# Attention and a squared-ReLU feed-forward: from one interleaved pass with one level of Strassen's form to three stages with two levels

## The chip, the core and the metric

The kernel runs on one core of one Trainium2 chip. The metric is the device time of one execution in microseconds (us). The engines are PE (matrix products), DVE, ACT and POOL (element work), and SP (which issues the transfers). PE writes only to PSUM, which has eight banks of 128 x 512 numbers; DVE and ACT read PSUM, POOL works from SBUF. All numbers are 32-bit floats.

## The reference

```python
scores = (1 / 8) * q @ k.T                          # 8 batches, 8 heads, 576 tokens, head size 64
thresh = max(scores, axis=-1) - tau
attn = softmax(where(scores >= thresh, scores, -1e9))
x = (attn @ v), heads side by side                  # 4608 tokens x 512
h = maximum(x @ w_in, 0)                            # w_in 512 x 2048
out = (h * h) @ w_out                               # w_out 2048 x 512
```

q, k and v arrive as 32-bit numbers, the two weights as 64-bit numbers, which the kernel converts itself.

## The kernel before, in words

**Attention** goes by pairs of heads (32 pairs) and blocks of query tokens: four blocks of 128 and one of 64 per pair, so 160 slots. In a slot, `scores` puts the score blocks of both heads into PSUM. `softmax` takes the row maximum (DVE, L342), the exponential (ACT, L356), the threshold with the row sum (DVE, L362) and the division (POOL, L378). `transposes` turns the weights (PE, L395 and L406) and copies them to SBUF (ACT, L397 and L407). `values` multiplies with v (PE, L432 and L437), for two blocks (256 tokens) or the last three (320 tokens) at a time, and ACT copies the result into x (L445). `turn` turns q and k of the next pair (L285, L294).

**The feed-forward** goes by pieces of 256 tokens, 18 in all. Each layer uses one level of Strassen's form: seven block products in place of eight. In `feed_forward`, the first layer (L491) has 14 products of 8 matmuls with 128 columns, the second (L600) seven of 8 matmuls with 256 columns. Sums of operands (`combine_x`, the sums of g) and of results run on DVE and POOL (helpers at L185 and L188), the square on POOL (L502) or DVE (L500). Nothing of this goes through DRAM.

**The order.** In the first 34 slots (`early_slot`) the order on PE, DVE, ACT and POOL is written out by hand: in nearly every slot one chunk of the weights is loaded and converted in six steps (`convert1` to `convert6`), and sums of weight blocks follow. The score tiles take two times three banks, all other PSUM tiles share two. After that only PE's order is written by hand; the scores take four banks and the others four. There `run` places feed-forward products between the slots, as many as keep a steady share, so that PE has products to do while DVE, ACT and POOL work on attention. A 32-bit matmul shows in the trace as two instructions, each with its weight load (PEld).

## Time and profile before

| what | value |
|---|---|
| median of 3 runs | 1578.9 us (1576.45 to 1580.72) |
| the profiled execution, its own time | 1579.66 us |
| its span | 1577.9 us |
| mean granted PE clock | 0.987 of full |
| 0 to 200 us: busy PE, DVE, ACT, POOL | 169.2, 155.7, 144.0, 158.0 us |
| 200 to 1480 us: the same | 1250.8, 647.1, 443.1, 428.3 us |
| clock in these two stretches | 0.95, 0.99 |

The profile's lines are read like this. In a timeline: start and duration in us, engine, line, operation, output tile <- inputs, shapes, number of instructions, and in brackets how long the engine stood idle before and what released it. In a list of groups: number of instructions, then total busy time and mean ns of one, then the idle time before them. Busy times of PE overlap, since an instruction's modelled end lies after the start of the next; the pace of PE is read from start to start.

### The profile page before, as it was taken

To read this page: it belongs to the slowest core of one execution; us is meant where nothing else is said; L and a number is where in the kernel's file an instruction comes from. 1 tells how busy PE (TensorE), PEld (TensorE's weight loads), DVE (VectorE), ACT (ScalarE), POOL (GpSimd) and SP (SyncE) were. 2 spreads that over 40 slices of the span, in tenths; PEclk is the share of its full clock that TensorE was granted. 3 is DMA by queue.
4 is the path that set the end of the run, shared out by engine and by line. 5 is a ranking of instruction groups with operands and counts; after the bars stand their busy time and mean duration, and the time that the engine had idled before them with its cause. 6 is when DMAs were issued, how large, how long until landed. Compare 5 with 4: busy or idle time off the path is not lost.

```text
span 1577.9 us, 25866 instructions
## 1 busy us (share of the span) xinstructions
PE 1511.6 (96%) x10042; PEld 1203.8 (76%) x10042; DVE 829.1 (53%) x1748; ACT 597.1 (38%) x1285; POOL 611.3 (39%) x690
## 2 busy tenths in 40 slices
PE   6888989999999999999999999999999999999998
PEld 3455557878786878787878786878788787878988
DVE  6878884636454455554554544454645464533222
ACT  6867743334242433333334333333334333421100
POOL 4899782423232242423242423241424242333221
PEclk9999989999999999999999999999999999999999
DMA  5544301010100100010001010001010001000000
GB/s 154 150 126 133 111 23 37 16 37 9 37 24 22 30 22 24 23 30 23 22 23 37 24 29 23 22 23 37 17 36 23 25 21 30 8 14 1 15 14 14
DMA packets 107914, 58.70 MB, mean 37 GB/s; under 512 B 89872, under 2 KB 99088, under 8 KB 107792
## 3 DMA queue, kind: packets, MB, share of 16 engines
q1 hardware_dynamic: 107792, 57.04, 13.0%
q8 instruction: 80, 1.31, 0.3%
q14 instruction: 42, 0.34, 0.1%
HBM read 47.58 MB, written 9.44 MB: 36 GB/s over the span
## 4 chain that ended last, share of the span: by engine, by line
PE 79%; DVE 7%; POOL 7%; ACT 4%; issue 2%; DMA 0%; SPq 0%; ACTq 0%; DVEq 0%; POOLq 0%
PE ph L491 28%; PE po L600 26%; PE sc L326 10%; PE pwT L406 6%; PE pv L437 4%; POOL w L378 3%; DVE nmx L342 3%; ACT w L356 2%; PE pwR L395 2%; PE pv L432 1%; PE pqk L285 1%; DVE g L185 1%; DVE s L188 1%; DVE w L362 1%; ACT x L445 1%
## 5 line engine op out<-in xcount | busy, mean ns | idle before, releaser
L378 POOL TENSOR_SCALAR w<-w,sm 128x576 f32<-128x576 f32 (+1 forms) x320 | 236.0, 748 | 575.8 <-DVE sm L369 561.9
L342 DVE TENSOR_REDUCE nmx<-sc 128x1 f32<-128x576 f32 x288 | 206.4, 749 | 190.1 <-PE sc L326 180.6
L362 DVE SCALAR_TENSOR_TENSOR w<-sc,thr,w 128x576 f32<-128x576 f32 x288 | 225.0, 814 | 138.8 <-ACT w L356 125.6
L356 ACT ACTIVATE w<-sc,nmx 128x576 f32<-128x576 f32 x288 | 199.8, 741 | 241.4 <-DVE nmx L342 234.7
L600 PE MATMUL po<-w_out,g 128*128 128x256 f32 x1152 | 267.7, 386 | 11.9 <-DVE g L185 9.6
L600 PEld LDWEIGHTS po<-w_out,g 128*128 128x128 f32 x1152 | 217.9, 193 | 43.6 <-issue 9.8
L491 PE MATMUL ph<-x,w_in 128*128 128x128 f32 x1728 | 208.8, 277 | 0.5
L326 PE MATMUL sc<-kT,qT 64*128 64x512 f32 (+3 forms) x1164 | 203.6, 464 | 2.6 <-DVE w L362 2.2
L491 PEld LDWEIGHTS ph<-x,w_in 128*128 128x128 f32 x1728 | 202.2, 193 | 3.2 <-ACT wR L401 1.3
L326 PEld LDWEIGHTS sc<-kT,qT 64*128 64x128 f32 (+1 forms) x1164 | 93.3, 176 | 105.4 <-issue 89.0
L406 PE MATMUL pwT<-ident,w 128*128 128x128 f32 x1024 | 145.6, 279 | 11.6 <-ACT x L445 9.4
L407 ACT COPY wT<-pwT 128x512 f32<-128x512 f32 x256 | 144.6, 591 | 29.1 <-PE pwT L406 26.3
L491 PE MATMUL ph<-xt,s_in 128*128 128x128 f32 x1152 | 142.9, 278 | 0.2
L437 PE MATMUL pv<-wT,va 128*64 128x320 f32 (+1 forms) x1024 | 141.3, 419 | 0.0
L491 PEld LDWEIGHTS ph<-xt,s_in 128*128 128x128 f32 x1152 | 136.3, 194 | 1.3 <-ACT wT L407 1.2
L406 PEld LDWEIGHTS pwT<-ident,w 128*128 128x128 f32 x1024 | 114.9, 142 | 27.1 <-ACT x L445 17.5
L188 DVE TENSOR_TENSOR u<-ph,u 128x512 f32<-128x512 f32 x110 | 75.7, 690 | 111.2 <-PE ph L491 105.4
L600 PE MATMUL po<-t_out,g 128*128 128x256 f32 x576 | 131.9, 379 | 0.0
L437 PEld LDWEIGHTS pv<-wT,va 128*64 128x64 f32 x1024 | 69.5, 139 | 65.1 <-issue 27.9
L600 PEld LDWEIGHTS po<-t_out,g 128*128 128x128 f32 x576 | 107.9, 190 | 13.8
L502 POOL TENSOR_TENSOR g<-p 128x512 f32<-128x512 f32 x36 | 38.1, 1059 | 155.1 <-ACT p L555 155.1
L188 DVE TENSOR_TENSOR o<-po,u 128x256 f32<-128x256 f32 x54 | 22.9, 424 | 96.2 <-PE po L600 96.2
(86 smaller groups left out, 1667.6 us busy)
## 6 DMA issues: line engine op xcount, KB each, us to landing
kn<-in_k_dram SPq DMA_DIRECT2D x72, 128.0 KB, 2.9
va<-in_v_dram SPq DMA_DIRECT2D x36, 256.0 KB, 2.7
out_dram<-o SPq DMA_DIRECT2D x36, 256.0 KB, 2.0
raw<-in_moe_w_in_dram SPq DMA_DIRECT2D x16, 512.0 KB, 4.1
raw<-in_moe_w_out_dram SPq DMA_DIRECT2D x16, 512.0 KB, 3.6
qn<-in_q_dram SPq DMA_DIRECT2D x56, 128.0 KB, 2.4
rn<-in_q_dram SPq DMA_DIRECT2D x36, 32.0 KB, 2.4
rn<-in_k_dram SPq DMA_DIRECT2D x36, 32.0 KB, 2.6
```

Source lines behind the costliest of these rows:

```text
L188: e.tensor_tensor(out=out, in0=x, in1=y, op=ALU.add)
L326: nc.tensor.matmul(to, qT[rows, ds(t * P, m)], kT[rows, ds(k0, n)], start=True, stop=True)
L342: nc.vector.tensor_reduce(out=nmx[:, j : j + 1], in_=sc[:, ds(at[j], S)], axis=AXIS.X, op=ALU.max, negate=True)
L356: nc.scalar.activation(out=w[:, ts(j, S)], in_=sc[:, ds(at[j], S)], func=AF.Exp, bias=nmx[:, j : j + 1], scale=1.0)
L362: nc.vector.scalar_tensor_tensor(out=w[:, ts(j, S)], in0=sc[:, ds(at[j], S)], scalar=thr[:, j : j + 1], in1=w[:, ts(j, S)], op0=ALU.is_ge, ...
L378: nc.gpsimd.tensor_scalar(out=out, in0=w, scalar1=r, scalar2=1.0, op0=ALU.mult, op1=ALU.mult)
L406: nc.tensor.transpose(pt[:, c, :], w[:, ds(j * (S + REST) + c * P, P)], ident[:, :])
L407: nc.scalar.copy(wT[:, j, :, at], pt[:, :, :])
L437: nc.tensor.matmul(pv[rows, :], va[:, j, c, :], wT[:, j, c, 0:n], start=False, stop=(c == FULL - 1), skip_group_check=True,)
L491: nc.tensor.matmul(to[:, j, :], a, b, start=(not more and j == 0 and c == 0), stop=(c == 1), skip_group_check=True,)
L502: e.tensor_tensor(out=to, in0=c[:, :, :], in1=c[:, :, :], op=ALU.mult)
L600: nc.tensor.matmul(to[:, :], a[:, f, :], b[:, f, :], start=(not more and f == 0), stop=(f == KF - 1), skip_group_check=True,)
```

## The change

The work is put into three stages, one after the other, and the order on all engines is written by hand.

1. All 160 slots of attention, with no feed-forward between them. The three-bank score tiles and two shared banks stay to the end. `values` now runs in every slot, for one block, and its result goes to DRAM (`xT`). A slot's steps are spread over four slots (`slot`). Weight conversions come every 2.5 slots, first w_out, later w_in. The sums of weight blocks for two levels (`sums`, 44 per weight) run on POOL, one per slot. The 49 sums of w_out are written to DRAM (`keep`), because both sets use the same SBUF tiles.
2. The first layer for all tokens, in nine steps of 512. Each step has seven outer products (`OUTER`) of seven inner ones (`inner`), 49 in all, each of four matmuls with 128 columns. Results of inner products are added on DVE, those of outer products on POOL (`final`, `add`). The sums of x for the next step run on POOL (`prepare_x`). ACT does ReLU and square, and the result is written to DRAM (`gT`). In the last step ACT's queue loads the w_out tiles back.
3. The second layer, again nine steps of 49 products of four matmuls with 128 columns. The squares are loaded (`load_g`), and 44 sums of them per step, outer and inner, go to POOL and, every third, to DVE (`adder`). The sums that the next step needs are issued in the last three outer products of a step.

The diff, cut (removed functions are those of the kernel before that the text above names: `feed_forward`, `combine_x`, `run`, `early_slot`):

```diff
+    OUTER, INNER = (1, 2, 6, 7, 4, 5, 3), (1, 6, 2, 7, 5, 4, 3)
+    SUMS_A = ((plus, 5, 7, 4), (minus, 6, 5, 1), (minus, 3, 2, 6), (minus, 7, 1, 7))
+    SUMS_B = ((minus, 5, 7, 1), (minus, 6, 3, 5), (minus, 4, 2, 6), (minus, 7, 3, 7))
+    AT_A, AT_B = ((1, 2), (7, 4)), ((1, 7), (2, 3))
...
+    def sums(W, which, at, done):
+        first = [at[a][b] for a in range(2) for b in range(2)]
+        for op, o, x, y in which:
+            for k_ in first:
+                to = W[o, k_] if o == y else weight_tile(W, o, k_)
+                yield op(nc.gpsimd, to[:, :], W[x, k_][:, :], W[y, k_][:, :])
+        for m in OUTER:
+            for op, o, x, y in which:
+                to = W[m, o] if o == y else weight_tile(W, m, o)
+                yield op(nc.gpsimd, to[:, :], W[m, x][:, :], W[m, y][:, :])
+            done(m)
...
+    def keep(m):
+        for k_ in INNER:
+            w_dram[m, k_] = dram.tile([P, BANK], FP32, name=f"w{m}{k_}")
+            later.append((w_dram[m, k_][:, :], W_OUT[m, k_][:, :]))
...
+    def values(i, t):
...
+        q0, n = t * P, BLK[t]
...
+        nc.tensor.matmul(pv[:, :], vd[:, :], wR[:, 0:n], start=False, stop=True, skip_group_check=True)
+        x = sb.tile([P, P], FP32, tag="x", bufs=3, name="x")
+        nc.scalar.copy(x[:, 0:n], pv[:, :])
+        later.append((xT[b][ts(hp, P), ds(q0, n)], x[:, 0:n]))
...
+    def slot(n):
...
+        values_and_load(n - 2)
+        turn_part(n - 1, "R")
+        stage(n + 2)
+        turn_part(n - 1, "W")
+        turn_part(n - 1, "w")
+        turn_begin(n)
+        stage(n + 1)
+        second(n + 1)
+        second(n + 2)
+        ahead(n + 3)
+        stage(n + 2)
+        second(n + 2)
+        turn_on(n, 0)
+        turn_on(n, 1)
+        stage(n + 1)
+        convert4(begun(3))
+        convert5(begun(3))
+        convert1(begun(1))
+        convert2(begun(1))
+        sums_step()
+        convert3(begun(2))
+        convert6(begun(4))
...
+    def inner(product, copy, temp, bank, final, tick):
...
+        X = bank()
+        product(X, 1, False)
+        p1 = temp("p1")
+        copy(p1, X)
+        tick(0)
+        Y = bank()
+        product(Y, 6, False)
+        u2 = temp("u2")
+        plus(nc.vector, u2, Y, p1)
+        tick(1)
+        product(X, 2, True)
+        final((0, 0), X, None)
+        tick(2)
+        Z = bank()
+        product(Z, 7, False)
+        u3 = temp("u3")
+        plus(nc.vector, u3, Z, u2)
+        tick(3)
+        W = bank()
+        product(W, 5, False)
+        final((1, 1), W, u3)
+        tick(4)
+        product(Z, 4, True)
+        final((1, 0), Z, u2)
+        tick(5)
+        product(W, 3, True)
+        final((0, 1), W, u2)
+        tick(6)
...
+    def prepare_x(n):
...
+        e = nc.gpsimd
+        for op, o, x, y in SUMS_B:
+            yield op(e, xo[:, o - 1, :, :], xo[:, x - 1, :, :], xo[:, y - 1, :, :])
...
+        for op, o, x, y in SUMS_B:
+            yield op(e, of[o], of[x], of[y])
...
+    def square(n, j, o):
+        nc.scalar.activation(out=o, in_=o, func=AF.Relu)
+        nc.scalar.activation(out=o, in_=o, func=AF.Square)
+        nc.sync.dma_start(out=gT[n][j][:, :].rearrange("p (k t) -> p k t", k=4), in_=o)
+    def squares_due(wait):
+        if squares and squares[0][0] + wait <= clock["n"]:
+            square(*squares.popleft()[1:])
...
+    def hidden_layer(n, also):
...
+            def product(to, k, more):
+                for j in range(4):
+                    nc.tensor.matmul(
+                        to[:, j, :], W_IN[m, k][:, ts(j, P)], of[k][:, m - 1, :], start=(not more and j == 0), stop=True,
+                        skip_group_check=True,
+                    )
+            def add(to, c, other, more, t=None):
+                if other is None:
+                    plus(nc.vector, to, c, more)
+                else:
+                    plus(nc.gpsimd, to, t, more)
+            def final(ab, c, other):
+                if m == 1:
+                    U2[ab] = tile4("u", 12)
+                    if other is None:
+                        nc.scalar.copy(U2[ab], c)
+                    else:
+                        plus(nc.vector, U2[ab], c, other)
+                    return
+                t = None
+                if other is not None:
+                    t = temp("t")
+                    plus(nc.vector, t, c, other)
+                if m == 6:
+                    add(U2[ab], c, other, U2[ab], t)
+                elif m == 7:
+                    U3[ab] = tile4("u", 12)
+                    add(U3[ab], c, other, U2[ab], t)
+                else:
+                    o = tile4("o", 8)
+                    add(o, c, other, U3[ab] if m in (4, 5) else U2[ab], t)
+                    if m == 5:
+                        add(U2[ab], c, other, U2[ab], t)
+                    row, col = {2: (0, 0), 4: (1, 0), 5: (1, 1), 3: (0, 1)}[m]
+                    squares.append((clock["n"], n, 4 * (2 * row + ab[0]) + 2 * col + ab[1], o))
+            def tick(at):
+                clock["n"] += 1
+                squares_due(4)
+                also(m, at)
+            inner(product, copy, temp, bank, final, tick)
...
+    def load_g(n):
+        for row, col in ((0, 0), (0, 1), (1, 1), (1, 0)):
+            for a, b in ((0, 0), (0, 1), (1, 1), (1, 0)):
+                t = gp.tile([P, 4, NQ], FP32, tag="g", bufs=36, name="g")
+                j = 4 * (2 * col + b) + 2 * row + a
+                nc.sync.dma_start(out=t[:, :, :], in_=gT[n][j][:, :].rearrange("p (k t) -> p k t", k=4))
+                operands[n, AT_A[row][col], AT_A[a][b]] = t
+                yield
+    turns = {"n": 0}
+    def adder():
+        turns["n"] += 1
+        return nc.vector if turns["n"] % 3 == 0 else nc.gpsimd
+    def outer_g(n):
+        for op, o, x, y in SUMS_A:
+            for a in range(2):
+                for b in range(2):
+                    k_ = AT_A[a][b]
+                    if o != y:
+                        operands[n, o, k_] = gp.tile([P, 4, NQ], FP32, tag="g", bufs=36, name="g")
+                    g = lambda m: operands[n, m, k_][:, :, :]
+                    op(adder(), g(o), g(x), g(y))
+                    yield
+    def inner_g(n, m):
+        for op, o, x, y in SUMS_A:
+            if o != y:
+                operands[n, m, o] = gp.tile([P, 4, NQ], FP32, tag="gi", bufs=6, name="gi")
+            g = lambda k_: operands[n, m, k_][:, :, :]
+            op(adder(), g(o), g(x), g(y))
+            yield
+    def output_layer(n, also):
...
+            def product(to, k, more):
+                g, w = operands[n, m, k], W_OUT[m, k].rearrange("p (k o) -> p k o", k=4)
+                for j in range(4):
+                    nc.tensor.matmul(
+                        to, g[:, j, :], w[:, j, :], start=(not more and j == 0), stop=(j == 3), skip_group_check=True
+                    )
...
+            def final(ab, c, other):
+                i = AT[ab]
+                mine = U3 if m in (4, 5) else U2
+                if m == 1:
+                    if other is None:
+                        nc.scalar.copy(U2[:, i, :], c)
+                    else:
+                        plus(nc.vector, U2[:, i, :], c, other)
+                elif other is None:
+                    if where:
+                        plus(nc.vector, place(ab), c, mine[:, i, :])
+                    if m in (5, 6):
+                        plus(nc.vector, U2[:, i, :], c, U2[:, i, :])
+                    if m == 7:
+                        plus(nc.vector, U3[:, i, :], c, U2[:, i, :])
+                else:
+                    plus(nc.vector, ts_[:, i - 1, :], c, other)
+                    if where:
+                        plus(nc.vector, place(ab), ts_[:, i - 1, :], mine[:, i, :])
+            inner(product, copy, temp, bank, final, lambda at: also(m, at))
+            if m in (5, 6):
+                plus(nc.vector, U2[:, 1:4, :], ts_[:, :, :], U2[:, 1:4, :])
+            if m == 7:
+                plus(nc.vector, U3[:, 1:4, :], ts_[:, :, :], U2[:, 1:4, :])
...
+            for n in range(-3, len(slots)):
+                slot(n)
+                if n == IN_SUMS:
+                    conv_stack.close()
+                    xpool = right.enter_context(tc.tile_pool(name="xpool", bufs=1, side="right"))
+                    load_x(0)
+                    xsums = prepare_x(0)
+                if n > IN_SUMS + 24 and n % 2:
+                    next(xsums, None)
...
+            acc = stack.enter_context(tc.tile_pool(name="acc", bufs=1))
+            banks = stack.enter_context(tc.tile_pool(name="banks", bufs=8, space=PSUM))
+            for n in range(NSTEP):
+                if n + 1 < NSTEP:
+                    load_x(n + 1)
+                    xsums = prepare_x(n + 1)
+                def also(m, at):
+                    if n + 1 < NSTEP:
+                        if m != 1 and at in (0, 1):
+                            next(xsums, None)
+                    elif at == 6:
+                        for k_ in INNER:
+                            t = weight_tile(W_OUT, m, k_)
+                            nc.scalar.dma_start(out=t[:, :], in_=w_dram[m, k_][:, :])
+                hidden_layer(n, also)
+            while squares:
+                squares_due(0)
+        right.close()
...
+            gp = stack.enter_context(tc.tile_pool(name="gp", bufs=1))
+            acc = stack.enter_context(tc.tile_pool(name="acc2", bufs=1))
+            banks = stack.enter_context(tc.tile_pool(name="banks2", bufs=8, space=PSUM))
+            for _ in load_g(0):
+                pass
+            for _ in outer_g(0):
+                pass
+            for _ in inner_g(0, 1):
+                pass
+            sums_in = iter(())
+            for n in range(NSTEP):
+                more = n + 1 < NSTEP
+                loads = load_g(n + 1) if more else iter(())
+                sums_g = outer_g(n + 1) if more else iter(())
+                def also(m, at):
+                    nonlocal sums_in
+                    i = OUTER.index(m)
+                    if at == 0:
+                        sums_in = inner_g(n, OUTER[i + 1]) if i < 6 else inner_g(n + 1, 1) if more else iter(())
+                    if i < 6 and at < 4 or i == 6 and at > 3:
+                        next(sums_in, None)
+                    if i == 6 and at == 6:
+                        next(sums_in, None)
+                    if i > 3 and (at > 2 if i == 4 else at > 0 if i == 5 else at < 6):
+                        next(sums_g, None)
+                    if at == 2:
+                        while later:
+                            to, from_ = later.popleft()
+                            nc.sync.dma_start(out=to, in_=from_)
+                    if at == 6:
+                        for k_ in range(1, 8):
+                            operands.pop((n, m, k_), None)
+                        for _ in range(4):
+                            next(loads, None)
+                output_layer(n, also)
```

## The prediction

> **What bounds the kernel now.** I read the page's head, then the chain that ended last, then timelines of stages that run alone, because the page's means mix stages.
>
> ```profile
> span 1577.9 us, 25866 instructions
> ...
> PE 1511.6 (96%) x10042; PEld 1203.8 (76%) x10042; DVE 829.1 (53%) x1748; ACT 597.1 (38%) x1285; POOL 611.3 (39%) x690
> ...
> PEclk9999989999999999999999999999999999999999
> ...
> PE 79%; DVE 7%; POOL 7%; ACT 4%; issue 2%; DMA 0%; SPq 0%; ACTq 0%; DVEq 0%; POOLq 0%
> ```
>
> PE is the bound: 96% busy and 79% of the chain. The others have room only because attention (heavy for DVE, ACT, POOL) is mixed with products (heavy for PE). So I need the pace of each kind of PE work; the tail shows the products alone:
>
> ```profile
> 1479.77 1.95 PE L491 MATMUL ph<-xt,s_in 128*128 128x128 f32 x16
> 1481.56 1.95 PE L491 MATMUL ph<-xt,w_in 128*128 128x128 f32 x16
> ...
> 1513.75 3.62 PE L600 MATMUL po<-t_out,s 128*128 128x256 f32 x16
> 1517.21 3.62 PE L600 MATMUL po<-t_out,g 128*128 128x256 f32 x16
> ```
>
> Start to start, 16 instructions (8 matmuls, two passes each) take 1.79 us at 128 columns, 111.7 ns apiece, and 3.46 us at 256. The two layers thus cost 18 x (14 x 1.787 + 7 x 3.455) = 885 us. A middle stretch prices attention the same way:
>
> ```profile
> 664.15 0.33 PE L395 MATMUL pwR<-ident,w 128*128 128x128 f32 x1
> 664.32 1.04 PE L406 MATMUL pwT<-ident,w 128*128 128x128 f32 x8
> 665.19 3.62 PE L600 MATMUL po<-t_out,s 128*128 128x256 f32 x16
> ...
> 673.42 0.70 PE L432 MATMUL pv<-wR,vdiag 128*128 128x256 f32 x2
> 674.05 1.95 PE L437 MATMUL pv<-wT,va 128*64 128x256 f32 x16
> 675.93 0.33 PE L395 MATMUL pwR<-ident,w 128*128 128x128 f32 x1
> ...
> 676.76 0.42 PEld L406 LDWEIGHTS pwT<-ident,w 128*128 128x128 f32 x4 [0.31 <-ACT x L445]
> ```
>
> Scores 1.23 us (644.50 to the transposes at 645.73), transposes 0.17 + 0.87, values 0.63 + 1.88 at 256 tokens and 0.74 + 2.31 at 320, turning q and k 1.07, a last block's scores and transposes 1.73. A pair of heads: 4 x 2.27 + 1.73 + 5.56 + 1.07 = 17.4 us, x 32 = 558. So 1443 us are work of PE and 135 are waits. The last line is a wait that grows with the change: transposes stand still until ACT has emptied the bank of the values.
>
> **Part 1, fewer products.** 9 steps x 49 products x 8 instructions x 111.7 ns = 394 us a layer, 788 for both: 97 us less. All of it lies on PE, so it counts, if the operands keep up.
>
> **Part 2, attention alone.** PE: scores in the three-bank form take 1.06 + 0.22 = 1.28 us (160.29 to 161.35, 154.35 to 154.57). Values now come block by block: 0.43 us less per 64 columns makes 1.02 at 128, and 0.41 for the rest, 1.43 a slot. A full slot is 1.28 + 1.04 + 1.43 = 3.75, a pair 4 x 3.75 + 2.73 + 1.07 = 18.8, x 32 = 602: 44 more than before. Waits: two banks instead of four. The values' copy starts 0.20 us after PE's next instruction (19.91 to 20.11 for such a copy), takes 0.275, and PE follows 0.05 later, less 0.17 of transposing the rest: 0.36 a slot, 58 us. The turn waits 0.41 for its bank, 13 us. DVE's loop (maximum 0.70, two threshold passes 1.55, small ones 0.2, maximum 0.70) is 3.2 of the 4.1 us slot, hidden; if PE were faster, it would be the next bound at 3.7 with its handoffs. ACT's 3.0 a slot is hidden, but a conversion's 1.36 queues ahead of the next slot's copies: 0.5 x 32 = 16. POOL has 2.2 + 1.27 (a weight sum) + 0.7, hidden within a slot. Start and drain 13 (the first scores start at 8.6). Sum 702. Loads, and the writes of weights and x to DRAM (SP issue 0.35 to 0.6 us each, waiting only for copies long issued), lie beside this. The first 200 us ran at a clock of 0.95 against 0.99 later; I charge nothing, since those slices held PE waits of 2 to 4 us that these slots lack. The Trainium skill (TensorE: Matmul & The Clock Gate, the HAM clock gate) says that an idle window of some 3.4 us halves the clock; the low rows would make 4% of 602, or 24 us more, the rule none within slots and, as an estimate, 1.7 us after one long gap.
>
> **Part 3, the first layer.** A product lasts 0.894 us and its consumer must free the bank within the next one: 0.20 + DVE 0.69 + 0.05 = 0.94, so 0.05 late once a pass: 63 passes, 3 us. Product 5 evicts twice from one bank, 0.5 x 9 = 5. POOL has 25 sums of 1.27 and four of 2.08 (by columns), 40 of a step's 44 us, hidden but late in products 4 and 5: 0.5 x 9 = 4. In the last step seven weight loads issue on ACT ahead of a copy that PE waits for: 7 x 0.35 (SP's issue) less 1.1 of room, x 6 = 8. Sum 394 + 20 = 414; upper bound, 0.1 us more per product, 44 more.
>
> **Part 4, between the layers.** Last eviction, sum, squares and write: 0.9 + 1.3 + 1.2 + 2.0 = 5.4. Then 16 loads, 4.2 MB: 27 us at the 154 GB/s of the first slice, 10 by the landing times (512 KB 3.6 us, 32 KB 2.5); I take 14, nearer the large loads. The weights' way back, 12.8 MB beside 4.2 MB of squares in the last step, needs 386 GB/s and may run into this gap; the upper end holds that. In other steps the added 95 GB/s are below the 154 already seen, hidden. Then 16 sums and two more, 16 us behind the last load. 35; ends 25 and 50. Nothing covers it.
>
> **Part 5, the second layer.** 44 sums of g a step, every third on DVE. Two adds with both inputs in SBUF do not run side by side:
>
> ```profile
> 1498.57 0.96 DVE L500 SCALAR_TENSOR_TENSOR g<-u 128x512 f32<-128x512 f32 x1
> 1498.94 1.17 POOL L185 TENSOR_TENSOR xt<-x,xt 128x256 f32<-128x256 f32 x1
> 1499.63 1.56 DVE L188 TENSOR_TENSOR s<-g 128x1024 f32<-128x1024 f32 x1
> 1500.08 2.01 POOL L502 TENSOR_TENSOR g<-c 128x512 f32<-128x512 f32 x1
> 1501.23 1.95 DVE L185 TENSOR_TENSOR g<-g 128x1024 f32<-128x1024 f32 x1
> ...
> L188 POOL TENSOR_TENSOR s_in<-w_in 128x512 f32<-128x512 f32 x4 | 5.1, 1280 | 0.0
> ```
>
> Alone these take 0.69, 0.73, 1.22, 1.04 and 1.22 (the shortest of each): 4.9 us of work in 4.6. In a step's last three outer products 28 sums are due: POOL 18.7 x 1.27 = 23.7, DVE 9.3 x 0.68 = 6.3, plus DVE's nine placements (0.29 by columns) and one long add, 3.1: 33 us in a window of 18.8 + 0.9. Less two sums that may come later, some 10 us late a step. Were the two engines free of each other, POOL's 23.7 would leave 4. I take 10, the row being the same kind of add: 8 x 10 = 80, sum 474. PE waits for operands there, DVE's evictions queue behind its sums. The Trainium skill (SBUF — State Buffer, Who interferes with whom) calls this an exclusive lock between GpSimd and a DVE instruction with two SBUF inputs; strictly so it would be 11 a step and 8 us more.
>
> **Sum.** 702 + 414 + 35 + 474 + 4 (end, as now) = 1629, plus the 1.8 us that the profiled execution's 1579.66 lies over its span: 1631. That execution is 0.05% from the median of 1578.9, so no correction. A forecast of +3.3%, its own range 1600 to 1665.
>
> **Rivals.**
> Attention packs better (the other side): copies hide, so that a pair costs PE's 18.8 to 19.8 us. Attention 615 to 647, total 1544 to 1576; it decides once a slot averages under 3.97 us against my 4.31. For it: the mixed middle spends 1300 - 392 - 387 = 521 us on 132 slots, 3.95. Against: four banks there, two here.
> The adds do not collide: layer two 426, total 1583. For it: POOL's 1.04 us squares kept their time beside DVE's evictions from PSUM; against: those read one SBUF input. With the first rival too, 1510.
> Attention is as slow as the first 180 us, (180 - 9 - 16) / 28 = 5.5 a slot with conversions in every one; halfway, 4.9, makes attention 797, total 1726. Against: POOL was full there, and here a conversion comes every 2.5 slots, for 80 slots.
>
> **How the numbers follow.** Forecast 0.42, all slower. Better packing 0.26: 0.21 faster, 0.05 same. No collision 0.12: 0.05 same, 0.07 slower. Both 0.05, faster. Slow slots 0.15, slower. Faster 0.26, same (within 0.3%, what measurement can tell) 0.10, slower 0.64. Range 1535 to 1700: below it both rivals and the best packing, above it most of the slow slots.
>
> **What would show it.** PE with 7056 product instructions; attention ending near 702 with PE about 86% busy and transposes waiting for ACT x; layer one at 46 us a step; a PE gap of 35 us; layer two at 53 us a step with PE waiting on POOL and DVE sums, stretched past 1.27 and 0.68. Wrong if slots fall under 4 us, or layer two keeps 44 to 47.

## The result, and the profile after

The changed kernel takes 1667.96 us (median of four, 1667.55 to 1668.32) where the kernel before takes 1579.02 (1576.45 to 1580.72): 1.0565 of it, 95% interval 1.0546 to 1.0583. Its profiled execution took 1667.85 us, with a span of 1666.0 and a mean PE clock of 0.976. From its page, in this order: the span, the busy times, PE's busy tenths and its clock over the span, and the shares of the chain that ended last.

```profile
span 1666.0 us, 34261 instructions
...
PE 1508.2 (91%) x12560; PEld 1255.7 (75%) x12560; DVE 1123.9 (67%) x2273; ACT 725.7 (44%) x1585; POOL 1180.9 (71%) x1231
...
PE   7999999999999999999999999996489988899888
...
PEclk9999999999999999999999999998699999999999
...
PE 67%; DVE 11%; ACT 8%; issue 6%; POOL 4%; DMA 2%; SPq 0%; ACTq 0%; DVEq 0%; POOLq 0%
```

PE's busy time is almost what it was (1511.6 before), though the layers' products were priced 97 us lower. Attention is busy 43 us more (669.4 us up to 730, against the 626 left before when the layers are taken off at their 885), and the two layers are busy some 50 us above their price (414.1 and 424.6 us for 394 each). PE's share of the span fell from 96% to 91%, and of the chain from 79% to 67%, with DVE, ACT and issue in its place. The stages, by the first and last product of each in the timeline:

| stage | forecast, us | measured, us |
|---|---|---|
| attention ends | 702 | 730.2 |
| first layer | 414 | 420.5 |
| gap to the second product of the second layer | 35 | 37.6 |
| rest of the second layer | 474 | 473 |

So the 37 us between forecast (1631) and result are attention's 28, 6 of the first layer and 3 of the gap.

**Attention.** PE in one full slot of the changed kernel and the start of the next (timeline):

```profile
696.60 1.13 PE L304 MATMUL sc<-kT,qT 64*128 64x512 f32 x4
697.66 0.49 PE L308 MATMUL sc<-kdiag,qT 128*128 128x128 f32 x2
698.08 1.09 PE L411 MATMUL pv<-wT,va 128*64 128x128 f32 x16
699.10 0.49 PE L414 MATMUL pv<-wR,vdiag 128*128 128x128 f32 x2
699.43 0.27 PE L368 MATMUL pwR<-ident,w 128*128 128x128 f32 x1
699.95 1.09 PE L381 MATMUL pwT<-ident,w 128*128 128x128 f32 x8 [0.25 <-ACT x L416]
700.97 0.70 PE L304 MATMUL sc<-kT,qT 64*128 64x512 f32 x2
```

Start to start: scores 1.06, their remainder 0.42, values 1.02 and 0.33, remainder's transpose with the wait 0.52, transposes 1.02. That is 4.37 us, where the forecast's pieces make 4.11. The wait (0.52 for 0.17 + 0.36) and the values on half of the array are as forecast; the remainder took 0.20 more, the transposes 0.15 more, the block-diagonal product 0.08 less. Both longer pieces end where PE goes from products on the whole array to products on half of it. PE's longest wait between 25 and 730 us, in all, number and longest:

```profile
PE pwT L381 <- ACT x L416: 40.6, 127, 0.8
```

**The first layer** keeps 45.8 us a step, and the last step, with the reload on ACT's queue, takes 7.5 more (53.3 us; a step is counted from the start of its first product to that of the next). The columns of this table by stretches are the window and its length, then busy time (and instructions) of PE, PEld, DVE, ACT and POOL, PE's clock, DMA share and GB/s:

```profile
776.00:822.00 46.00, 45.81 (x396) 44.79 (x395) 28.98 (x43) 23.55 (x42) 39.38 (x30) 1.00 0.34 115
...
1097.00:1151.00 54.00, 49.06 (x399) 47.08 (x398) 29.55 (x43) 24.92 (x44) 27.63 (x23) 0.97 0.85 294
```

**The gap and the second layer** (two cuts of the timeline). PE waits 10.82 us for a load of g and 24.69 for the sums. Later, at the end of a step, DVE's sums and POOL's alternate:

```profile
1161.74 2.05 PE L709 MATMUL po<-w,g 128*128 128x128 f32 x8 [10.82 <-DMA g<-g]
1188.48 2.07 PE L709 MATMUL po<-w,gi 128*128 128x128 f32 x8 [24.69 <-DVE gi L93]
...
1428.21 0.56 DVE L96 TENSOR_TENSOR u<-t,u 128x384 f32<-128x384 f32 x1
...
1432.09 4.27 POOL L96 TENSOR_TENSOR g<-g 128x512 f32<-128x512 f32 x3
...
1432.91 1.04 DVE L96 TENSOR_TENSOR o<-t,u 128x128 f32<-128x128 f32 x1
...
1435.16 1.75 DVE L96 TENSOR_TENSOR g<-g 128x512 f32<-128x512 f32 x1
...
1442.07 2.08 PE L709 MATMUL po<-w,g 128*128 128x128 f32 x8 [3.50 <-DVE u L96]
...
1443.94 1.60 PE L709 MATMUL po<-w,gi 128*128 128x128 f32 x8
```

An addition of 128x128 from SBUF lasts 1.04 us beside POOL's, a sum of 128x512 1.75. At 1442.07 PE has waited 3.50 us for DVE, and the next eight instructions take 1.87 us from start to start in place of 0.89: the clock has dropped (0.50 from 1441.7 to 1445.1). PE's longest wait from 1195 us on:

```profile
PE po L709 <- DVE u L96: 38.5, 21, 3.5
```

### The profile page after: what moved, and what is told of

The parts are those of the page before. It is cut to its first block, busy times and chain, and to the rows that moved or that the text cites. A ratio compares the mean times of both kernels' runs of the same rounds, so it can differ in the third digit from the quotient of the medians.

```text
span 1666.0 us, 34261 instructions
## 1 busy us (share of the span) xinstructions
PE 1508.2 (91%) x12560; PEld 1255.7 (75%) x12560; DVE 1123.9 (67%) x2273; ACT 725.7 (44%) x1585; POOL 1180.9 (71%) x1231
## 4 chain that ended last, share of the span: by engine, by line
PE 67%; DVE 11%; ACT 8%; issue 6%; POOL 4%; DMA 2%; SPq 0%; ACTq 0%; DVEq 0%; POOLq 0%
PE ph L610 24%; PE po L709 16%; PE sc L304 8%; PE pwT L381 7%; PE pv L411 6%; PE sc L308 3%; PE pv L414 3%; ACT w L332 2%; DVE w L337 2%; ACT x L416 2%; DVE o L96 2%; POOL g L93 2%; DVE g L93 1%; PE pqk L266 1%; DVE u L96 1%
## 5 line engine op out<-in xcount | busy, mean ns | idle before, releaser
L709 PE MATMUL po<-w,g 128*128 128x128 f32 x2016 | 271.2, 284 | 55.0 <-DVE u L96 38.5
L96 DVE TENSOR_TENSOR t<-ph,t 128x512 f32<-128x512 f32 x288 | 199.1, 691 | 153.0 <-PE ph L610 127.0
L709 PEld LDWEIGHTS po<-w,g 128*128 128x128 f32 x2016 | 250.7, 199 | 61.2 <-DVE u L96 43.1
L610 PE MATMUL ph<-xo,w 128*128 128x128 f32 x2016 | 251.1, 278 | 5.1 <-ACT t L548 4.7
L610 PEld LDWEIGHTS ph<-xo,w 128*128 128x128 f32 x2016 | 236.2, 193 | 6.6 <-ACT t L548 5.7
L709 PE MATMUL po<-w,gi 128*128 128x128 f32 x1512 | 209.2, 283 | 30.5 <-DVE gi L93 27.4
L709 PEld LDWEIGHTS po<-w,gi 128*128 128x128 f32 x1512 | 191.9, 199 | 33.6 <-DVE gi L93 28.2
L610 PE MATMUL ph<-xi,w 128*128 128x128 f32 x1512 | 203.2, 279 | 1.7 <-DVE t L96 1.7
L381 PE MATMUL pwT<-ident,w 128*128 128x128 f32 x1152 | 161.1, 280 | 44.2 <-ACT x L416 40.6
L610 PEld LDWEIGHTS ph<-xi,w 128*128 128x128 f32 x1512 | 183.9, 192 | 10.7 <-DVE t L96 3.5
L304 PE MATMUL sc<-kT,qT 64*128 64x512 f32 (+2 forms) x768 | 187.1, 578 | 5.4 <-DVE w L337 4.3
```

Of the source, the lines that this page charges most:

```text
L96: e.tensor_tensor(out=out, in0=x, in1=y, op=ALU.add)
L304: nc.tensor.matmul(to, qT[rows, ds(t * P, m)], kT[rows, ds(k0, n)], start=True, stop=True)
L381: nc.tensor.transpose(pt[:, c, :], w[:, ds(j * (S + REST) + c * P, P)], ident[:, :])
L610: nc.tensor.matmul(to[:, j, :], W_IN[m, k][:, ts(j, P)], of[k][:, m - 1, :], start=(not more and j == 0), stop=True, skip_group_check=True,)
L709: nc.tensor.matmul(to, g[:, j, :], w[:, j, :], start=(not more and j == 0), stop=(j == 3), skip_group_check=True)
```

## The experiments

The theory: attention is set by the wait for the bank that ACT empties and by changes of the array's form; the second layer by the sums of g, whose two engines shut each other out. The main rivals: another engine bounds the slot; the two engines are free of each other; PE itself is slower in these forms.

### The sums of g left out

```diff
-                        operands[n, o, k_] = gp.tile([P, 4, NQ], FP32, tag="g", bufs=36, name="g")
-                    g = lambda m: operands[n, m, k_][:, :, :]
-                    op(adder(), g(o), g(x), g(y))
+                        operands[n, o, k_] = operands[n, x if o == 5 else 2, k_]
```

The same in `inner_g`.

> The second layer leaves out the sums of g (11 blocks of one row and one column of Strassen's sums, 44 additions of 128x512 a step): its products read a loaded block of the same size in their place, so that this part of the result is not computed. The sums over products, the products and the loads stay. Theory (the second layer is set by DVE and POOL, which add fp32 blocks of SBUF and shut each other out): the layer falls from 474 us to about 400 (394 of products and the ends), the whole from 1668 to about 1594, and DVE's additions of two SBUF operands, 0.77 us on the mean now, fall to the 0.29 us that the same size takes with one operand in PSUM. Rival (the products themselves are slower in this layer's form, or the granted clock is lower there, whatever is added beside them): the layer stays above 450 us and the whole above 1644.

1564.4 us (1564.2 to 1564.6), 0.990 of the kernel before (0.987 to 0.993). A stretch of the second layer and DVE's additions:

```profile
1230.00:1280.00 50.00, 50.00 (x450) 50.00 (x449) 19.55 (x64) 2.39 (x9) 0.00 (x0) 1.00 0.30 106
```

```profile
L96 DVE TENSOR_TENSOR o<-t,u 128x128 f32<-128x128 f32 x108 | 31.6, 292 | 3.7
```

PE is never idle, 0.111 us an instruction, and the layer lasts 397 us from its first product. Of the 104 us saved, 78 are the layer's and 25 the second wait of the gap; the expectation had counted only the layer. PE is as fast in this form as priced, so the rival falls: what the second layer takes above its products is the sums'. Without them the changed kernel is 1% faster than the kernel before. They are not the whole account of the 89 us lost. The products give 97 us back and the sums take 104; by difference, an estimate, about 82 more are lost elsewhere: attention alone takes 37 us above the 693 of its work on PE and of all waits before, the first layer 27 above its products, the gap 13 without the wait for sums, and the end 5. No run kept the layers between the slots of attention with two levels, so what the split into stages costs by itself is not shown.

### Who makes the sums

Two thirds on DVE in place of one third, and all of them on DVE:

```diff
-        return nc.vector if turns["n"] % 3 == 0 else nc.gpsimd
+        return nc.gpsimd if turns["n"] % 3 == 0 else nc.vector    # first run
+        return nc.vector                                         # second run
```

> The sums of g in the second layer are dealt out the other way: two thirds to DVE (0.68 us each alone) and one third to POOL (1.27 us each alone), where the changed kernel gives DVE one third. Nothing else changes. If the two engines shut each other out when both read two SBUF operands, their times add: the sums of a step take 44 x (2/3 x 1.27 + 1/3 x 0.68) = 47 us before and 44 x (1/3 x 1.27 + 2/3 x 0.68) = 38.6 us after, so a step gets about 4 to 8 us shorter: the layer goes from 474 to about 410 to 440, the whole to 1604 to 1635. Rival (the engines are free of each other and the longer one alone bounds the step): POOL's share falls from 37 to 19 us a step and DVE's rises by 10 us to about 45; with PE at 44 us a step the layer falls to about 400 to 410 and no addition of DVE is longer than 0.75 us. Second rival (neither; the loads or the clock set the step): the layer stays within 10 us of 474.

> All sums of g in the second layer go to DVE, none to POOL, in the places that they have. Theory (a DVE addition of two SBUF operands is long only while POOL reads SBUF): the means fall to what they are alone, 0.68 us for 128x512 (0.68 to 1.57 now), 0.29 for o<-t,u of 128x128 (0.80 now) and 0.56 for 128x384 (1.01 now); DVE then has 44 x 0.68 + 18 = 48 us a step and is the longest engine, the layer 440 to 480 us and the whole 1635 to 1675. Rival (the additions are long by SBUF traffic of PE and the DMAs): the means stay above 1.0 and 0.5 us, DVE would have 44 x 1.0 + 21 = 65 us a step, the layer near 590 and the whole near 1780.

Two thirds: 1673.6 us (1673.0 to 1674.2), slower by 6, where 1604 to 1635 was expected; in size this is the second rival (loads or clock), which the second run refutes. All: 1626.5 (1625.8 to 1627.3), faster by 41 and below the 1635 to 1675 expected. The group of 128x128 additions, and for the second run also sums of g (groups of the whole span for the changed kernel and for all on DVE, of 1180 to 1560 us for two thirds):

```profile
L96 DVE TENSOR_TENSOR o<-t,u 128x128 f32<-128x128 f32 x108 | 82.7, 766 | 3.7
L93 DVE TENSOR_TENSOR g<-g 128x512 f32<-128x512 f32 x57 | 77.3, 1358 | 2.3 <-POOL g L93 2.3
```

```profile
L96 DVE TENSOR_TENSOR o<-t,u 128x128 f32<-128x128 f32 x81 | 41.0, 507 | 2.8
```

```profile
L93 DVE TENSOR_TENSOR g<-g 128x512 f32<-128x512 f32 x171 | 115.1, 682 | 0.0
...
L96 DVE TENSOR_TENSOR o<-t,u 128x128 f32<-128x128 f32 x108 | 31.6, 292 | 3.7
```

The mean of the small addition goes 766, 507, 292 ns as POOL's share goes 2/3, 1/3, 0, and a sum of g falls from 1358 to 682 ns. Traffic of PE and the DMAs was the same or denser, so POOL is the cause: shown. The count of the step was wrong in the first run: on the mean of the second to the eighth it went from 53.1 to 54.2 us. The times of the two engines don't simply add to the step. DVE's queue also holds, between those sums, the additions that empty PE's banks. With two thirds of the sums in that queue, and a sum of g still 1.04 us long on the mean, PE's waits for DVE's t rose from 2.6 to 16.4 us, and those for u stayed at 35 (38.5 in the changed kernel). With POOL out, the waits for u fall to 16.1 and the clock is 1.00 in six of seven stretches of the layer:

```profile
PE po L709 <- DVE u L96: 16.1, 23, 1.4
```

### Spread over the step

Three quarters of the sums on DVE, the outer sums from the fourth outer product on:

```diff
-        return nc.vector if turns["n"] % 3 == 0 else nc.gpsimd
+        return nc.gpsimd if turns["n"] % 4 == 0 else nc.vector
...
-        for op, o, x, y in SUMS_A:
+        for op, o, x, y in (SUMS_A[0], SUMS_A[3], SUMS_A[1], SUMS_A[2]):
...
-                    if i > 3 and (at > 2 if i == 4 else at > 0 if i == 5 else at < 6):
+                    if i == 3 or i == 4 and at > 1 or i == 5 and at > 2:
                         next(sums_g, None)
...
-                        for _ in range(4):
+                        for _ in range(8):
                             next(loads, None)
```

> Three quarters of the sums of g go to DVE and one quarter to POOL, and the 16 outer sums of the next step are issued from the fourth outer product on in place of the last three (with their loads two products earlier and in another order), so that no stretch of a step holds many more sums than another. The dealing alone, two thirds to DVE, had left the step at 53 us: there DVE was busy 42 of 53 us and POOL 20, DVE waited for PE 93 us and PE for DVE 51 us in the layer. Theory (the sums stand in DVE's queue ahead of the additions that free PE's results, in bunches): spread out, PE's waits for DVE shrink to under 20 us in all, a step falls to 45 to 47 us and the layer to about 405 to 425, the whole to about 1600 to 1620. Rival (the sum of the two engines' exclusive times sets the step, wherever it stands): 33 x 0.68 + 11 x 1.27 + the sums of outputs 18 = 54 us a step as before, the layer stays at 465 to 475 and the whole at 1660 or more.

1646.3 us (1646.1 to 1646.4), a step of 51.2 us on the mean of the second to the eighth: between the two. Spreading and dealing gave 22 us, half of what taking POOL out gave with the sums left in their bunch.

### The start of the second layer

Ahead of the first product only the inner sums. In this kernel the outer sums of the first step read a block that the inner sums have overwritten, which changes that step's result and not the work.

```diff
-            for _ in outer_g(0):
-                pass
             for _ in inner_g(0, 1):
                 pass
+            sums_0 = outer_g(0)
...
+                    if n == 0 and i == 0:
+                        for _ in range(4 if at == 6 else 2):
+                            next(sums_0, None)
```

> Only the start of the second layer is touched: ahead of its first product there are the inner sums of the first outer block alone, and the outer sums of the first step are issued beside the products of that block. Theory (the second part of the gap, 24.7 us in which PE waits for a DVE addition, is the queue of the outer sums that are placed ahead of what the first product reads): the gap falls from 37 to about 15 to 20 us and the whole from 1668 to about 1648 to 1652. Rival (the loads of g are late in any case: the first part of the gap, 10.8 us, is a wait for a load, and the remaining ones come after it): the wait moves to the DMA and the gap stays above 30 us. The first step of the layer gets the additions that were ahead of it and may be up to 10 us longer, which would be paid back out of the gap.

1663.9 us (1662.1 to 1665.7). PE in the timeline:

```profile
1164.81 2.05 PE L709 MATMUL po<-w,g 128*128 128x128 f32 x8 [10.76 <-DMA g<-g]
1170.21 2.08 PE L709 MATMUL po<-w,gi 128*128 128x128 f32 x8 [3.35 <-POOL gi L93]
...
1196.48 2.08 PE L709 MATMUL po<-w,g 128*128 128x128 f32 x8 [7.84 <-DVE u L96]
```

The second product starts 18 us earlier, the last 2 us earlier. The cause of the long wait is the one named, but the sums are only put off: the first step waits for DVE in its turn (7.84 us at 1196) and runs at a clock of 0.64 and 0.87 in its first stretches. The expectation allowed 10 us of payback; it was 16, so 4 us were gained of the 16 to 20 expected.

### Edits for the second layer together

First run: the spread, the earlier start (with four sums ahead) and the reload on SP's queue. Second run: all sums on DVE, 16 outer sums four at a time beside the third to the sixth outer product, the earlier start and the reload.

```diff
...
-                            nc.scalar.dma_start(out=t[:, :], in_=w_dram[m, k_][:, :])
+                            nc.sync.dma_start(out=t[:, :], in_=w_dram[m, k_][:, :])
...
-                    if i > 3 and (at > 2 if i == 4 else at > 0 if i == 5 else at < 6):
+                    if 1 < i < 6 and at in ((1, 2, 4, 5) if i < 4 else (0, 2, 4, 5)):   # second run
...
```

> All edits at once that aim at the second layer: three quarters of the sums on DVE, spread over the step; ahead of the first product only four outer sums and the first inner ones, the other twelve beside the first outer product; and the reload of the second layer's weights in the last step of the first layer is issued on SP's queue in place of ScalarE's. Theory (three separate causes, which add): the spread brings about 50 us if the theory of its own run holds, the gap about 15 us less a part paid back in the first step, the reload 6 to 8 us in the last step of the first layer (54 us there against 45.8 in the others): about 1590 to 1600. Rival (the first step only gets the sums that stood ahead of it, as in the run with the gap alone, and the reload is hidden by other waits): within 5 us of the run with the spread alone.

> What the earlier runs pointed to, together: all sums of g on DVE; the 16 outer sums of the next step four at a time beside the third to the sixth outer product, with the loads put in the order that this needs; ahead of the first product three inner sums, then the four outer sums whose block the inner ones overwrite, the other twelve beside the first two outer products; the reload of the second layer's weights on SP's queue. Theory (DVE has 44 x 0.60 + 18 = 44 us a step at its pace of one sum per 0.60 us, so spread evenly it just fits beside PE's 43.8): a step falls from 48.4 (all on DVE) to 44 to 46 us, 20 to 40 us in nine steps; the gap gives 10 to 15 us, the reload 6 to 8: from 1626.5 to 1565 to 1590. Rival (what spreading gave with both engines came from fewer collisions, not from the even spread): the steps stay at 48 us and only the gap and the reload count, 1605 to 1612.

The first: 1644.4 us (1643.8 to 1645.0), 2 less than the spread alone, so the rival. On SP's queue the last step of the first layer is 8 us shorter (46.0 for 53.9), but the wait for g that follows is 16.1 us in place of 11.2, and the first step pays back the rest. The second: 1603.4 us (1600.6 to 1605.7), 1.014 of the kernel before (1.0125 to 1.016), the best version found, and not better than before: just under its rival's 1605 to 1612, and above its theory's 1565 to 1590. Stretches of 53 us in the second layer, of the changed kernel, of all on DVE and of this run:

```profile
1346.00:1399.00 53.00, 47.22 (x396) 46.21 (x396) 40.20 (x74) 2.12 (x8) 42.27 (x31) 0.97 0.28 100
```

```profile
1346.00:1399.00 53.00, 49.89 (x433) 48.56 (x432) 44.88 (x109) 2.12 (x8) 0.00 (x0) 1.00 0.29 101
```

```profile
1346.00:1399.00 53.00, 50.72 (x442) 49.58 (x441) 46.92 (x117) 2.33 (x9) 0.00 (x0) 1.00 0.30 100
```

On the mean of the second to the eighth a step is 53.1, 48.8 and 47.3 us. The spread itself gave only 1.5 us a step, 12 us in the eight steps behind the first: DVE is busy 46.92 of 53 us and has little left. The other 10 of the 22 us between the two profiled executions came ahead of the second step: the second product of the layer comes at 1163.5 in place of 1182.8, but the first step then waits longer (6.69 us for a sum of g at 1173.93) and ends only 10 us earlier.

### The order in a slot

```diff
-        values_and_load(n - 2)
         turn_part(n - 1, "R")
+        values_and_load(n - 2)
```

> Attention alone is touched: in each slot the second half of the previous slot's transposes is issued ahead of the values' transposes, so that the ScalarE copy that frees the shared PSUM bank has one product group more (about 1 us) to finish. Theory (the shared bank and its copy are on the path; in the changed kernel the transposes wait 0.36 us a slot for it, and 152 such waits sum to 78.5 us at the weight loads): the wait falls from 0.36 to at most 0.1 us, the full slot from 4.37 to about 4.12 us, the end of attention from 730 to about 693 us (150 slots x 0.25 = 37), the whole from 1668 to about 1631. Rival (the wait only shows that ScalarE, or the switch between whole-array and row- or column-wise products, bounds the slot): the wait moves to another place of the slot and the end of attention falls by less than 10 us, so the whole stays above 1655.

1664.4 us (1660.9 to 1668.0), attention ends at 729.0. PE in a full slot and ahead of it (timeline), and PE's longest waits between 25 and 730 us:

```profile
694.92 1.09 PE L411 MATMUL pv<-wT,va 128*64 128x128 f32 x16 [0.80 <-ACT kT L276]
...
697.38 1.13 PE L304 MATMUL sc<-kT,qT 64*128 64x512 f32 x4
...
701.42 1.13 PE L304 MATMUL sc<-kT,qT 64*128 64x512 f32 x4
```

```profile
PE pv L411 <- ACT kT L276: 27.0, 31, 2.3
PE pv L411 <- ACT kT L269: 21.1, 30, 2.3
```

A full slot does lose its wait: 4.04 us in place of 4.37, more than forecast. But in the two slots of each pair that turn q and k, the values now need the bank that ACT empties for kT, and wait 48.1 us in all where the transposes had waited 40.6. The total follows the rival, the place follows the theory: with two banks, whoever comes next waits for ACT. Exchanging the order only in slots without a turn was not tried.

### One more change of the array's form, twice a slot

```diff
-                    pv[rows, :], va[:, j, c, :], wT[:, j, c, 0:n], start=(c == 0), stop=False, skip_group_check=True
+                    pv[rows, :], va[:, j, c, :], wT[:, j, c, 0:n], start=(c == 0), stop=(c == FULL - 1), skip_group_check=True
...
+            if c == FULL // 2 - 1:
+                nc.tensor.matmul(pv[:, :], vd[:, :], wR[:, 0:n], start=False, stop=False, skip_group_check=True)
-        nc.tensor.matmul(pv[:, :], vd[:, :], wR[:, 0:n], start=False, stop=True, skip_group_check=True)
```

> Attention alone is touched: in each slot the one whole-array product of the values (wR by the block-diagonal values, 128 rows and columns) is issued between the fourth and the fifth of the eight chunks, in place of behind them. No product is added; the array goes twice more from whole-array to column-wise products and back. Theory (the slot of 4.37 us against 4.11 as forecast is longer by the change of the array's form, 0.15 to 0.20 us at each): 2 x 0.15 to 2 x 0.20 us more a slot, 45 to 60 us over the 150 slots, less the wait of the transposes for the copy that it may fill (0.36 us a slot before): the end of attention at 745 to 790 us. Rival (a change of form costs nothing, the longer rows are only how overlapping products are recorded): the end of attention stays within 8 us of 730.

1686.1 us (1685.8 to 1686.5), attention ends at 748.2, 18 us later:

```profile
701.27 0.66 PE L411 MATMUL pv<-wT,va 128*64 128x128 f32 x8
701.86 0.49 PE L415 MATMUL pv<-wR,vdiag 128*128 128x128 f32 x2
702.28 0.66 PE L411 MATMUL pv<-wT,va 128*64 128x128 f32 x8
702.86 0.33 PE L368 MATMUL pwR<-ident,w 128*128 128x128 f32 x1
703.30 0.66 PE L381 MATMUL pwT<-ident,w 128*128 128x128 f32 x4
```

The same products take 1.59 us (701.27 to 702.86) in place of 1.35: 0.24 for two changes, 0.12 each on the mean; the whole-array product itself takes 0.42 with column-wise products next, in place of 0.33. 0.08 of the 0.24 fills the wait for the copy (0.44 to the transposes in place of 0.52), and 0.16 a slot is left: an ordinary pair of five slots takes 22.49 us in place of 21.67. Pairs with weight conversions grow less (22.81 for 22.18), which leaves the 18 us measured. The rival falls; the size expected, 0.15 to 0.20, was too large. The Trainium skill (TensorEngine Tiling (Array Packing), Key Properties) says that changing the tiling mode drains TensorE; it gives no figure, and these runs agree with it.

### The copy of the values elsewhere

Made by DVE, and, in another run, kept on ACT with the values' product in a scores tile:

```diff
-        nc.scalar.copy(x[:, 0:n], pv[:, :])
+        nc.vector.tensor_copy(x[:, 0:n], pv[:, :])                              # first run
-        pv = bank([P, n], "pv")
+        host = hosts.pop(slots.index((i, t)) + 4, None)                         # second run
+        pv = bank([P, n], "pv") if host is None else host[:, ds(BANK + P, n)]
...
```

> Attention alone is touched: the copy of the values out of the shared PSUM bank is made by DVE in place of ScalarE (0.3 us each). Theory (the copy is late because it stands in ScalarE's queue behind the exponentials and the conversions, and the transposes of the next weights wait for that bank): the wait of the transposes for the copy, 40.6 us at the matmuls, falls under 15 us, and the end of attention from 730 to between 695 and 715, the whole to 1635 to 1655. Rival (DVE's queue, 0.75 us of maximum and two thresholds of 0.81 us a slot, holds it as long, or the wait goes to the next tenant of the two banks as in the run with the order exchanged): the end of attention stays within 10 us of 730 and the wait appears under DVE's name or another's.

> Attention alone is touched: the values' product no longer takes one of the two shared PSUM banks; it is written into 128 columns of the middle bank of a scores tile, which the scores leave unused. No instruction is added. Theory (two banks are too few for four tenants a slot, the values, the remainder's and the two halves' transposes, so that PE waits for a ScalarE copy wherever the order puts it): with one tenant less the transposes' wait of 40.6 us at the matmuls falls under 10 us without going elsewhere, the slot loses 0.25 to 0.35 us, and the end of attention comes at 680 to 700, the whole at 1620 to 1640. Rival (the chain through ScalarE bounds the slot, whatever the banks): the wait moves to the values' product or the scores and the end of attention stays within 10 us of 730. Second rival (the values' product now waits for the readers of the scores' tile): attention gets longer, 740 or more.

1809.8 us (1806.7 to 1813.0) and 1860.8 (1857.4 to 1864.3); attention ends at 869.2 and 921.4. Lines from the list of all waits, one of each run:

```profile
DVE x L416 <- PE pv L414: 312.0, 159, 3.5
```

```profile
DVE nmx L320 <- ACT x L417: 390.3, 156, 5.1
```

In the first, DVE's queue stands still about 2 us a slot until PE has made the values, with the softmax of later slots behind it: both theories missed that the copy is not only late in a queue but holds one up. The second is its second rival: the maximum of the scores waits for the copy of other columns of the same bank. The Trainium skill (PSUM — Partial Sum Buffer, PSUM bank collisions raise a hardware error) says that the compiler adds such a dependency between any two engines on one bank and quadrant, reads too; the 390 us agree, though the trace does not show what put the wait there. So no run shows what a third bank would give.

A last run put this place of the values together with the edits of the run at 1603, with the outer sums spread finer, and was lost with it:

> The values' place in the scores tile together with the sums on DVE, the earlier start of the second layer and the reload on SP's queue; and the 16 outer sums are spread finer: two beside the second outer product, three beside each of the next four, two beside the last (the run before had four beside the third to the sixth, where DVE then had 8 x 0.60 + 2.6 = 7.4 us for 6.25 us of products). Theory (both edits hold): attention gives the 30 to 50 us of the run with the values' place alone, a step falls from 46.9 to 45 to 46 us, 8 to 15 us in nine steps: 1603 less 38 to 65, 1538 to 1565, under the kernel before. Rival (ScalarE's chain bounds attention): 1588 to 1600, above the kernel before.

1796.1 us (1794.0 to 1798.5). Its first layer starts at 918.6. The second took 47.6 us a step, so the finer spread gave nothing.

## Why the prediction was right, and where it was not

The direction and most mechanisms held. The result is 37 us above the forecast, 3 above the forecast's own range (1600 to 1665) and inside the range stated (1535 to 1700). Two cuts of the kernel before, on which the account of part 2 rests (timeline):

```profile
80.30 1.09 PE L406 MATMUL pwT<-ident,w 128*128 128x128 f32 x8
...
81.32 1.13 PE L326 MATMUL sc<-kT,qT 64*128 64x512 f32 x4
...
154.35 0.49 PE L330 MATMUL sc<-kdiag,qT 128*128 128x128 f32 x2
154.57 0.14 PEld L395 LDWEIGHTS pwR<-ident,w 128*128 128x128 f32 x1
154.68 0.27 PE L395 MATMUL pwR<-ident,w 128*128 128x128 f32 x1
```

- **Part 1** held: without the sums the second layer's products take 0.111 to 0.112 us an instruction, as forecast.
- **Part 2**, attention, is the mis-sized term: 702 forecast, 730 measured. The bank wait of 0.36 a slot is right to 0.01. PE is busy 92% of the stage where 86% was forecast: its own pieces were read too short, not the waits.
  - The remainder of the scores was priced at 0.22, up to 154.57. That is the start of the next weight load; the next product starts at 154.68, so the piece takes 0.33.
  - Both pieces were read where products on the whole array come next (0.33, and 0.87 for eight transposes). Here they take 0.42 and 1.02, with products on half of the array next. The kernel before had such a row for the transposes too: 1.02 from 80.30 to 81.32. The 0.09 of the remainder is what the experiment with one more change of form shows for a like product (0.42 for 0.33). The 0.15 of the transposes is of the size of its changes, but was not tested by itself.
  - An ordinary pair takes 21.7 us in place of 21.0, 20 us in 32 pairs. The sixteen pairs with conversions are longer by 10 us in all (22.18 us for most, up to 22.66 beside the weight sums) and the last four by 4, where the forecast had 16 for conversions.
  - The other 10 us are the start. For start and drain 13 us were forecast, but the first weights are transposed only at 25.06. Until then the score products of a slot run at half clock (2.74 us) and, from the third slot on, come 5.2 us apart, waiting for DVE. No run tested that.
- The rival that attention packs better was priced by slots under 3.97 us on the mean. The slots of an ordinary pair take 4.33, and with the exchanged order 4.31; its full slot alone, 4.04, is still not there.
- **Part 3** held: 420.5 for 414, with 45.8 a step for 45.1 and the reload's 7.5 for 8. Most of what the reload cost was not to be had back: 5 of the 7 to 8 us went to the next load.
- **Part 4** held, 35.5 us of waits for 35, and split as worked out: POOL's first sum starts 19.9 us behind the last product, when its load has landed (19.4 forecast for evictions, squares, writes and loads), and the sums follow, 17.7 us to PE's second product (16 forecast).
- **Part 5** held in its sum, 473 for 474, partly by luck: one term was too large and one was left out. The additions lengthen each other as forecast (1.04 to 1.75 us), and the exclusive lock that the prediction cited agrees: no addition of DVE is long once POOL has none. But the listed waits of PE come to 49 us (38.5 for u, the rest below 4 each), and to 62 with those too short for that list, counted from the start of one product to the next; 80 was forecast. The other 17 us are the clock, priced at nothing: it is at half in 38 of the layer's 473 us, where 163 instructions take 0.22 us each in place of 0.11. The slow products behind the 3.50 us wait agree with the clock gate that the prediction cited for attention. The length of a wait alone does not decide it here, though: half clock also follows waits of 1.83 us (at 1505.50), 1.86 (at 1495.31) and, in attention, 1.60 (at 672.03), while the wait of 3.08 us at 1398.46 is followed by full clock.
- The rival that the additions do not collide is refuted by the run without POOL.

## What to carry to other kernels

Count the element work of a cheaper algorithm on the engine that must also empty PE's banks, and not only the products saved: here 97 us of products were won, and 104 us went to sums, before anything that the split into stages may cost. Where two engines share such work, look whether their long additions stretch each other before dealing them out; one engine alone was 41 us faster than two. Price a PE instruction from a row with the same neighbours, since what comes before and after changes its cost, and count from the start of a product to the start of the next product, not of its weight load.

## What was not expected of the hardware

- Beside POOL's sums a 128x128 DVE addition from SBUF takes 0.77 us on the mean and 0.29 without them, while the same size with one operand in PSUM keeps 0.29 in both.
- Two changes between whole-array and column-wise products cost 0.24 us a slot.
- The wait that an exchange of order takes from one product comes back at the next tenant of the bank at nearly the same total, 48.1 us for 40.6.
- Half clock for 3.4 us follows waits of PE of 1.60, 1.83 and 1.86 us, and one of 3.08 us is not followed by it.
